# Part of the inverse's correction on TensorE sums, shorter scans and moved tests in a gated recurrence with a mixture of experts

## The chip, the cores and the metric

The kernel runs on one core of a Trainium2 chip. The metric is the device time of one launch in microseconds (us). The engines are called PE (TensorE), DVE (VectorE), ACT (ScalarE), POOL (GpSimd) and SP (SyncE, which issues transfers).

## What is computed

First a recurrence over 768 steps for each of 4 x 8 (batch, head) pairs, with a complex gate per step and channel whose magnitude is cut to 0.999; then each token of 384 values goes to its best one of 8 experts.

```python
mag = np.sqrt(a_re * a_re + a_im * a_im)
scale = np.minimum(mag, 0.999) / (mag + 1e-06)
a_re_n, a_im_n = (a_re * scale, a_im * scale)
for t in range(S):                     # S = 768, state 48 x 48, complex
    S_re, S_im = ar * S_re - ai * S_im + kv, ar * S_im + ai * S_re
    y[:, :, t] = np.einsum('bhd,bhde->bhe', q[:, :, t], S_re)
...
h = np.maximum(np.einsum('ecd,edf->ecf', disp, w1), 0.0)
y = np.einsum('ecf,efd->ecd', h, w2)   # top-1 routing, scaled by the gate
```

## The kernel before

**Scan.** The 768 steps are cut into chunks of 96. The 256 rows (batch, head, chunk) form two groups g = 0, 1 of 128 partitions. For each group DVE scans products of the complex gates backward over the 96 steps, in seven blocks j of 8, 16, 16, 16, 16, 16 and 8 steps (`scan_ops`). A step is a `mul` (L221) and an `add` (L232). It is issued as one instruction each (a whole step) where another operation stands between the two, and as two half-width instructions each where not, since the second half then covers the first one's result.

**Norm.** Before block j can be scanned, its gates are normalised (`norm_ops`, eleven operations): xa, squares on ACT (L162) written into the tile `a4`; xb, their sums by PE with the identity (tile `xp`, L135; four passes for eight steps, eight for sixteen); xc, on ACT Ln, Exp and Square for each half (L177 to L179); t5, a scaled copy on ACT (tile `t5n`, L184); then on DVE m (L190, one per half), c1 (tile `c0n`, L193), s (L197), and two mul into `a4` (L202). c1 writes in place into `c0n`, which t5 reads.

**Post.** Of a scanned block `post_ops` makes q and k scaled by the products and by their inverse: wa, squares on ACT (L257); wb, sums on PE (tile `wp`, L135); wc, Ln and Exp on ACT, the reciprocal v0 (L272, L273); kw on DVE (L276); m (L281, one per half), x times v0; nu (L284), (m − 2)·v0, a correction step of the reciprocal; gq (L288), −nu·q; qw (L292), followed by a store to memory by POOL (tile `scr`).

**Order.** `dve_ops` writes DVE's order: during the scan of block j stand the norm of block j+1 (g = 0: of block j+1 and after) and the post of block j−1, at fractions of the block given in `NORM_AT` and `POST_AT`. In the first group ACT's and PE's orders come from the framework. `a4` has three buffers (`p_a4`), shared by the blocks of both groups in turn: norm k+2 takes the buffer of post block k−1. From the second group's start on, 32 attention units (a batch and a chunk) run between the scan steps, with all engines in an order by hand (`SLOT` tables; a unit's operations are placed every 10.25 us of DVE cost). A unit loads the stored q and k (tile `qkc`), transposes on PE, multiplies, carries the state (L385: a copy for the first chunk, an add after). PSUM tag `tr` has two buffers. Then come the routing and the experts, where PE does three passes for each product.

**Tests.** `pend_test` (L312 to L315) and `uncovered` test on DVE whether the values are in the range that the method covers; the flag is used late in the expert part.

Of the kernel before, what the change touches and what calls it, by code (L numbers as in the profile page):

```python
# [18 lines left out]
C = 96  # L19
# [22 lines left out]

# [17 lines left out]


class Att:


    def __init__(self, const, c_att, tc, dram, ident, q, k, v, a_re, a_im):
# [142 lines left out]
    def scan_ops(self, g, j):  # L208

        nc = self.nc  # L210
        ops = []
        for s in range(SIZES[j] - 1, -1, -1):
            st = {}

            def mul(cs=slice(0, D), s=s, st=st):
                a4 = self.a4[g, j]
                if 'xy' not in st:
                    st['xy'] = self.p_t.tile([128, 4, D], F32, tag="xy", name=f"xy_{g}_{j}_{s}")
                w = a4[:, s + 1, 0:2, cs]
# [17 lines left out]
            ops += [(mul, lambda f=mul: halves(f), .27), (add, lambda f=add: halves(f), .16)]  # L237
        return ops


    def post_ops(self, g, j):
# [49 lines left out]
        def qw():  # L291
# [36 lines left out]
    def unit(self, b, c):  # L328
# [49 lines left out]
        def add():  # L378

            if not last:  # L380
# [54 lines left out]
    def slots(self):  # L435
# [8 lines left out]
        for n in range(-2, len(us) + 3):  # L444
            for i, (t, o) in enumerate(SLOT if n < ALONE - 1 else SLOT_A if n < ALONE else SLOT_B):
                if 0 <= n + o < len(us):
                    ops.append((n + i / len(SLOT), us[n + o][t], cost.get(t, 0)))
        return ops

    def dve_ops(self, slots, t0, dt):  # L450
# [9 lines left out]
        for k, (g, j) in enumerate(sl):  # L460
# [772 lines left out]
def uncovered(nc, const, sums, smalls, route, out):  # L1233


    bad = const.tile([128, 5], F32, name="bad")
    nc.vector.memset(bad, 0.0)
    for g in range(2):
        ok = const.tile([128, 2, NSUM], F32, name=f"ok{g}")
        sv = sums[g]  # L1240
        nc.vector.tensor_scalar(out=ok[:, 0], in0=sv[:, 0], scalar1=1e5, scalar2=None, op0=ALU.is_lt)
        nc.vector.tensor_scalar(out=ok[:, 1], in0=sv[:, 1], scalar1=1e4, scalar2=None, op0=ALU.is_lt)
        m = const.tile([128, 1], F32, name=f"okm{g}")
        nc.vector.tensor_reduce(out=m, in_=ok.rearrange("p z j -> p (z j)"), op=ALU.min, axis=AX.X)
        nc.vector.tensor_tensor(out=m, in0=m, in1=smalls[g], op=ALU.mult)
        nc.vector.tensor_scalar(out=bad[:, g:g + 1], in0=m, scalar1=-1.0, scalar2=1.0, op0=ALU.mult, op1=ALU.add)
    m = const.tile([C, 1], F32, name="okf")
    nc.vector.tensor_reduce(out=m, in_=route.fine, op=ALU.min, axis=AX.X)
    nc.vector.tensor_scalar(out=bad[:C, 2:3], in0=m, scalar1=-1.0, scalar2=1.0, op0=ALU.mult, op1=ALU.add)
    nc.vector.tensor_reduce(out=bad[:C, 3:4], in_=route.over, op=ALU.max, axis=AX.X)  # L1250
    nc.vector.tensor_reduce(out=bad[0:1, 4:5], in_=route.narrow, op=ALU.max, axis=AX.X)
    one = const.tile([128, 1], F32, name="one")
    nc.vector.memset(one, 1.0)
# [11 lines left out]
def kernel(ctx, tc, q, k, v, a_re, a_im, w_gate, w1, w2, out):  # L1265
# [6 lines left out]
    with ExitStack() as c_main, ExitStack() as c_att:  # L1272
# [102 lines left out]
```

## Time and profile before

| | before |
|---|---|
| runs, us | 674.98, 675.65, 678.44 (median 675.65) |
| profiled execution, us | 671.0, its span 669.3 |
| mean granted PE clock | 0.92 of full |
| busy of the span | PE 81%, DVE 72%, ACT 52%, POOL 14% |
| chain that ended last, by engine | PE 60%, DVE 23%, ACT 8%, DMA 4% |

Rows of a timeline give the start in the span, the duration, the line, the operation, what it writes and reads, and in brackets the idle time before it and what ended that. Times on one engine overlap by some hundredths: what an instruction costs is the distance from its start to the next one's. PE passes that follow each other are shown as one row (x8). The granted clock is in parts of the full 2.4 GHz; .50 is the lower level of 1.2 GHz. A window's row gives its bounds and length, the busy time and (x count) of each engine, the clock, and the transfers' share and GB/s.

The scan of the first group takes the first 130 us, that of the second with its attention units some 170 more, the experts the rest.

### The profile page before, as it was taken

Reading aid. Unit: us, or ns where it says so; the run is one execution under the profiler, and the core shown is the slowest. Engines: PE = TensorE matmul, PEld = TensorE weight load, DVE = VectorE, ACT = ScalarE, POOL = GpSimd, SP = SyncE. Lnnn points to the kernel's source line nnn. Section 1 sums busy time; section 2 is a strip of 40 time slices with the busy share of each in tenths; the row PEclk is TensorE's granted clock in tenths of the full one; section 3 lists DMA queues with packets and bytes.
Section 4 is the critical chain, followed back from the end, with each engine's and each line's share of the span. In section 5 each row is a group of like instructions: output and inputs, shape, how many; then the busy total and the mean of one; then the engine's idle time right before and its main releaser. Section 6 shows DMA issues by size and latency. Waiting matters only on the chain.

```text
span 669.3 us, 12570 instructions
## 1 busy us (share of the span) xinstructions
PE 544.7 (81%) x4455; PEld 472.1 (71%) x4455; DVE 479.7 (72%) x1428; ACT 345.4 (52%) x789; POOL 92.8 (14%) x140
## 2 busy tenths in 40 slices
PE   0344434248798999899999999999999999999994
PEld 0122212126587877789999888899999999999993
DVE  5999999999999999827657776465455545564531
ACT  7456534476788886544554553244444443443420
POOL 8030000000000000101322221101120202021111
PEclk9776656676899999989999999999999999999998
DMA  5299444596659777776988742583535362636101
GB/s 189 66 319 324 165 165 138 192 224 201 193 163 252 189 180 223 248 152 160 217 228 226 179 111 70 156 252 92 171 94 176 104 182 92 201 88 200 35 35 35
DMA packets 73239, 111.89 MB, mean 167 GB/s; under 512 B 6402, under 2 KB 63045, under 8 KB 71888
## 3 DMA queue, kind: packets, MB, share of 16 engines
q1 hardware_dynamic: 66384, 77.13, 42.7%
q0 software_dynamic: 6784, 33.88, 15.0%
q8 instruction: 37, 0.61, 0.4%
q14 instruction: 34, 0.28, 0.1%
HBM read 72.99 MB, written 34.26 MB: 160 GB/s over the span
## 4 chain that ended last, share of the span: by engine, by line
PE 60%; DVE 23%; ACT 8%; issue 4%; DMA 4%; POOL 1%; SPq 0%; POOLq 0%; DVEq 0%; ACTq 0%
PE ph L981 15%; PE my L989 14%; DVE xy L221 5%; PE tr L354 4%; PE pa L362 4%; DVE a L232 4%; PE s L375 3%; PE y L418 3%; DVE qko L292 2%; PE x L610 2%; PE y L423 2%; DVE a L202 2%; PE xp L135 2%; PE my L1003 2%; PE wp L135 2%
## 5 line engine op out<-in xcount | busy, mean ns | idle before, releaser
L135 PE MATMUL xp<-a,ident 128*128 128x384 f32 x84 | 48.2, 739 | 90.2 <-ACT a L162 90.2
L880 DVE TENSOR_TENSOR lo<-raw,hi 128x384 fp32r<-128x384 f32 (+2 forms) x128 | 66.5, 553 | 65.5 <-ACT hi L879 55.9
L135 PEld LDWEIGHTS xp<-a,ident 128*128 128x128 f32 x84 | 23.0, 289 | 110.1 <-ACT a L162 78.3
L879 ACT CAST hi<-raw 128x384 fp32r<-128x384 f32 (+2 forms) x128 | 60.0, 512 | 55.1 <-PE ph L981 42.5
L221 DVE TENSOR_TENSOR xy<-a 128x96 f32<-128x96 f32 (+1 forms) x299 | 74.6, 279 | 0.6
L354 PE MATMUL tr<-ident,qkc 96*96 96x96 f32 x512 | 65.6, 252 | 11.0 <-DMA qkc<-scr 6.9
L981 PE MATMUL ph<-xh,hi 128*128 128x448 f32 (+4 forms) x192 | 69.7, 365 | 1.1 <-DVE hl L1027 0.9
L981 PE MATMUL ph<-xl,hi 128*128 128x448 f32 (+4 forms) x192 | 67.8, 353 | 0.0
L981 PE MATMUL ph<-xh,lo 128*128 128x448 f32 (+4 forms) x192 | 67.7, 353 | 0.0
L1027 DVE SCALAR_TENSOR_TENSOR hl<-ph,hh 128x448 fp32r<-128x448 f32 (+4 forms) x64 | 37.4, 586 | 39.0 <-ACT hh L1026 37.9
L1026 ACT ACTIVATE hh<-ph 128x448 fp32r<-128x448 f32 (+4 forms) x64 | 32.8, 514 | 61.0 <-PE ph L981 60.6
L989 PE MATMUL my<-hl,hi 128*128 128x448 f32 (+4 forms) x168 | 60.2, 358 | 0.0
L354 PEld LDWEIGHTS tr<-ident,qkc 96*96 96x96 f32 x512 | 47.6, 129 | 17.5 <-issue 6.7
L989 PE MATMUL my<-hh,lo 128*128 128x448 f32 (+4 forms) x168 | 59.9, 356 | 0.0
L989 PE MATMUL my<-hh,hi 128*128 128x448 f32 (+4 forms) x168 | 56.1, 360 | 0.1
L232 DVE TENSOR_TENSOR a<-xy 128x48 f32<-128x48 f32 (+1 forms) x296 | 55.1, 215 | 0.4
L362 PE MATMUL pa<-qT,kT 128*96 128x96 f32 x512 | 54.8, 251 | 0.0
L362 PEld LDWEIGHTS pa<-qT,kT 128*96 128x96 f32 x512 | 50.6, 168 | 1.4 <-issue 1.0
L954 POOL DMA_INDIRECT out_dram<-o,xr x26 | 28.9, 1111 | 157.7 <-DVE o L953 155.9
L630 POOL DMA_INDIRECT disp<-x,idx x32 | 30.1, 939 | 116.5 <-DVE idx L629 64.7
L418 PE MATMUL y<-a_sb,v 128*64 128x96 f32 x512 | 42.3, 253 | 2.3 <-ACT lt L621 1.7
L375 PE MATMUL s<-v,qkc 128*96 128x96 f32 x448 | 44.1, 253 | 0.0
(196 smaller groups left out, 1187.4 us busy)
## 6 DMA issues: line engine op xcount, KB each, us to landing
raw<-in_moe_w_dram SPq DMA_DIRECT2D x64, 384.0 KB
qkc<-scr SPq DMA_DIRECT2D x32, 528.0 KB
scr<-qko POOLq DMA_DIRECT2D x10, 1536.0 KB, 6.9
disp<-fill POOLq DMA_DIRECT2D x7, 772.0 KB, 17.6
v<-in_v_dram SPq DMA_DIRECT2D x32, 144.0 KB
xr<-disp SPq DMA_DIRECT2D x6, 675.5 KB
sx<-s SPq DMA_DIRECT2D x56, 72.0 KB
a<-in_a_re_dram SPq DMA_DIRECT2D x10, 384.0 KB
```

The costliest lines, as they stand in the source:

```text
L135: nc.tensor.matmul(out=pt[:, :m], lhsT=self.ident, rhs=t[:, h:h + m], start=i == 0, stop=i == 1)
L221: nc.vector.tensor_tensor(out=st['xy'][:, :, cs].rearrange("p (u z) d -> p u z d", u=2), in0=crossed(a4[:, s, 1, cs]), in1=w, op=ALU.mult)
L232: nc.vector.tensor_tensor(out=o, in0=xy[:, 0:4:2, cs], in1=xy[:, 1:4:2, cs], op=ALU.add)
L354: nc.tensor.transpose(out=pt[:, h * C:h * C + C], in_=qk(slice(0, C), 4 * hh + h, slice(z_ * C, z_ * C + C)), identity=self.ident[:C, :C])
L362: nc.tensor.matmul(out=pa[:, h * C:h * C + C], lhsT=kT[:, 4 * hh + h], rhs=qT[:, 4 * hh + h], start=True, stop=True)
L375: nc.tensor.matmul(out=ps[:, h * D:h * D + C], lhsT=qk(slice(None), h, slice(C, 2 * C)), rhs=v[:, h * D:h * D + C], start=True, stop=True)
L418: nc.tensor.matmul(out=py[o:o + DP, i // 2 * C:i // 2 * C + C], lhsT=v[:, h * D:h * D + DP], rhs=a_sb[:, h, :], start=True, stop=c == 0)
L879: nc.scalar.copy(out=hi[i][:, s], in_=raw[i][:, s])
L880: nc.vector.tensor_tensor(out=lo[i][:, s], in0=raw[i][:, s], in1=hi[i][:, s].bitcast(F32), op=ALU.subtract)
L981: nc.tensor.matmul(out=ph[:, :WIDTHS[e]], lhsT=a[:, k, fs], rhs=r[:, k, :WIDTHS[e]], start=k == 0 and i == 0, stop=k == KT - 1 and i == 2)
L989: nc.tensor.matmul(out=py[m][:, :WIDTHS[e]], lhsT=a[:, f % self.PF, ms], rhs=r[:, :WIDTHS[e]], start=f == 0 and i == 0, stop=f == NF - 1 a ...
L1027: nc.vector.scalar_tensor_tensor(out=hl[:, :w], in0=ph[:, :w], scalar=0.0, in1=hh[:, :w].bitcast(F32), op0=ALU.max, op1=ALU.subtract)
```

## The change

In the first group nu is made by PE: into a PSUM tile `nu` of tag `tr` go −2·v0 (with a new constant matrix `minus2`) plus m by the identity, where m is now x·v0². ACT makes v0² by a new Square for each half. gq reads PSUM in two halves. The second group keeps DVE's nu.

In block 0 of both groups the first scan step falls away, as its factor is one: the step after reads the swapped values, and two ACT copies write what stood there. The fractions for the first group are new, and some of the second's. `pend_test(0)` goes from the second group's first block to the end of the scans; the range tests go from before the experts into the expert part, where the flag is summed; the state copy of a first chunk goes from DVE to ACT (four of them); the unit spacing is 10.1.

```diff
-NORM_AT = [(-.25, -.15, .012, .012, .43, .25, .376, .45, .52, .611, .711)] * NS + \
+NORM_AT = [(-.25, -.15, .012, .012, .52, .472, .503, .535, .628, .66, .691)] * NS + \
...
-POST_AT = [(0, .138, .138, 0, .42, .421, .55, .55, .68)] * NS + \
+POST_AT = [(0, .138, .138, .441, .566, .597, .61, .722, .753, .785)] * NS + \
...
+        self.minus2 = const.tile([128, 128], F32, name="minus2")
+        nc.gpsimd.tensor_scalar(out=self.minus2, in0=self.ident, scalar1=-2.0, scalar2=None, op0=ALU.mult)
...
-        for s in range(SIZES[j] - 1, -1, -1):
+        top = SIZES[j] - 1
+        for s in range(top - (j == 0), -1, -1):
+            turned = j == 0 and s == top - 1
...
-                w = a4[:, s + 1, 0:2, cs]
+                w = swapped(a4[:, s + 1, 1, cs]) if turned else a4[:, s + 1, 0:2, cs]
...
+                if turned and cs.start == 0:
+                    a = self.a4[g, j][:, top]
+                    nc.scalar.copy(out=a[:, 0], in_=a[:, 1])
+                    nc.scalar.mul(out=a[:, 1], in_=a[:, 2], mul=-1.0)
...
+                if sums:
+                    nc.scalar.activation(st['o'][:, i, 0, 1], v0[:, i], AF.Square)
...
-                nc.vector.tensor_tensor(out=st['m'][:, i], in0=x, in1=st['v0'][:, i], op=ALU.mult)
+                nc.vector.tensor_tensor(out=st['m'][:, i], in0=x, in1=st['o'][:, i, 0, 1] if sums else st['v0'][:, i], op=ALU.mult)
+
+        def nu_sums():
+            st['nu'] = []
+            for x, i in st['xs']:
+                pt = self.ps.tile([128, 8, D], F32, tag="tr", name=f"nu_{g}_{j}_{i.start}", bufs=2)
+                m = i.stop - i.start
+                nc.tensor.matmul(out=pt[:, :m], lhsT=self.minus2, rhs=st['v0'][:, i], start=True, stop=False)
+                nc.tensor.matmul(out=pt[:, :m], lhsT=self.ident, rhs=st['m'][:, i], start=False, stop=True)
+                st['nu'].append((pt[:, :m], i))
+
+        def gq_of(k):
+            for x, i in st['nu'][k:k + 1]:
+                nc.vector.scalar_tensor_tensor(out=st['v0'][:, i], in0=x, scalar=-1.0, in1=st['in'][:, 0, i],
+                                               op0=ALU.mult, op1=ALU.mult)
...
-                    nc.vector.tensor_copy(out=ss, in_=psv)
+                    nc.scalar.copy(out=ss, in_=psv)
...
-                at.append((0.56, .8, lambda: (self.pend_copy(0), self.pend_test(0), self.pend_cols(0))))
+                at.append((0.56, 0, lambda: (self.pend_copy(0), self.pend_cols(0))))
...
-        out += [lambda: self.pend_copy(1), lambda: self.pend_test(1), lambda: self.pend_cols(1)]
+        out += [lambda: self.pend_copy(1), lambda: self.pend_test(1), lambda: self.pend_test(0), lambda: self.pend_cols(1)]
...
-                ops = att.dve_ops(slots, 6.5, 10.25)
+                ops = att.dve_ops(slots, 6.5, 10.1)
```

DVE, the last part of scan block 2 of the first group, before, with c1 of norm 3 (`c0n_3`) and the end of post block 1 (`qko_1`, `v_0_1`):

```order
L193 SCALAR_TENSOR_TENSOR c0n_3_397<-lnn_3_396,c0n_3_397 128x768
L221 TENSOR_TENSOR xy_2_7_464<-a_0_2_211 128x192
L197 SCALAR_TENSOR_TENSOR t5n_3_398<-c0n_3_397,t5n_3_398 128x768
L232 TENSOR_TENSOR a_0_2_211<-xy_2_7_464 128x96
L284 SCALAR_TENSOR_TENSOR v_0_1_425<-qko_1_393,v_0_1_425 128x768
L221 TENSOR_TENSOR xy_2_6_470<-a_0_2_211 128x192
L288 SCALAR_TENSOR_TENSOR v_0_1_425<-v_0_1_425,qkin_1_252 128x768
L232 TENSOR_TENSOR a_0_2_211<-xy_2_6_470 128x96
L202 TENSOR_TENSOR a_0_3_364<-a_3_263,t5n_3_398 128x16x48
L221 TENSOR_TENSOR xy_2_5_476<-a_0_2_211 128x4x24 x2
L232 TENSOR_TENSOR a_0_2_211<-xy_2_5_476 128x2x24 x2
L292 TENSOR_TENSOR qko_1_393<-a_0_1_152,v_0_1_425 128x16x96
```

The same part after the change:

```order
L206 SCALAR_TENSOR_TENSOR c0n_3_394<-lnn_3_393,c0n_3_394 128x768
L236 TENSOR_TENSOR xy_2_6_467<-a_0_2_209 128x192
L303 TENSOR_TENSOR qko_1_391<-wp_1_0_416,qko_1_391 128x8x48
L251 TENSOR_TENSOR a_0_2_209<-xy_2_6_467 128x96
L303 TENSOR_TENSOR qko_1_391<-wp_1_8_419,qko_1_391 128x8x48
L236 TENSOR_TENSOR xy_2_5_479<-a_0_2_209 128x192
L210 SCALAR_TENSOR_TENSOR t5n_3_395<-c0n_3_394,t5n_3_395 128x768
L251 TENSOR_TENSOR a_0_2_209<-xy_2_5_479 128x96
L215 TENSOR_TENSOR a_0_3_361<-a_3_262,t5n_3_395 128x16x48
L236 TENSOR_TENSOR xy_2_4_485<-a_0_2_209 128x192
L215 TENSOR_TENSOR a_0_3_361<-a_3_262,t5n_3_395 128x16x48
L251 TENSOR_TENSOR a_0_2_209<-xy_2_4_485 128x96
```

and right behind these:

```order
L316 SCALAR_TENSOR_TENSOR v_0_1_422<-nu_1_0_473,qkin_1_250 128x384
L236 TENSOR_TENSOR xy_2_3_491<-a_0_2_209 128x192
L316 SCALAR_TENSOR_TENSOR v_0_1_422<-nu_1_8_476,qkin_1_250 128x384
L251 TENSOR_TENSOR a_0_2_209<-xy_2_3_491 128x96
L328 TENSOR_TENSOR qko_1_391<-a_0_1_154,v_0_1_422 128x16x96
```

Both m (now L303) have moved behind `c0n`, nu is gone, and gq (L316) is two instructions that read `nu_1`; qw (L328) is the last of the stretch, as L292 is before.

ACT, norm 3 and post block 1, from the last Ln of xp to t5, before:

```order
L177 ACTIVATE lnn_3_396<-xp_3_8_376,b_tiny 128x384
L178 ACTIVATE c0n_3_397<-lnn_3_396,b_lncap 128x384
L272 ACTIVATE v_0_1_425<-wp_1_0_419,b_tiny 128x384
L179 ACTIVATE lnn_3_396,sums_82<-c0n_3_397 128x384
L273 ACTIVATE v_0_1_425<-v_0_1_425 128x384
L272 ACTIVATE v_0_1_425<-wp_1_8_422,b_tiny 128x384
L273 ACTIVATE v_0_1_425<-v_0_1_425 128x384
L184 ACTIVATE t5n_3_398<-c0n_3_397,b_half 128x768
L204 ACTIVATE a_0_3_364<-a_0_3_364 128x16x48
```

and after the change:

```order
L190 ACTIVATE lnn_3_393<-xp_3_8_374,b_tiny 128x384
L191 ACTIVATE c0n_3_394<-lnn_3_393,b_lncap 128x384
L292 ACTIVATE v_0_1_422<-wp_1_0_416,b_tiny 128x384
L192 ACTIVATE lnn_3_393,sums_84<-c0n_3_394 128x384
L293 ACTIVATE v_0_1_422<-v_0_1_422 128x384
L292 ACTIVATE v_0_1_422<-wp_1_8_419,b_tiny 128x384
L295 ACTIVATE qko_1_391<-v_0_1_422 128x8x48
L293 ACTIVATE v_0_1_422<-v_0_1_422 128x384
L295 ACTIVATE qko_1_391<-v_0_1_422 128x8x48
L197 ACTIVATE t5n_3_395<-c0n_3_394,b_half 128x768
L217 ACTIVATE a_0_3_361<-a_0_3_361 128x16x48
```

Two Squares (L295) into `qko_1` now stand between the first Exp of v0 (L293) and t5 (`t5n_3`, now L197).

PE, the end of the first group (`wp_5` and `nu_6` belong to its last two post blocks, `xp_1` and `xp_2` to norms 1 and 2 of the second group, `pt` is made by pend_cols), before:

```order
L135 MATMUL wp_5_0_917<-qko_5_897,ident 128x384 x2
L135 MATMUL wp_5_8_920<-qko_5_897,ident 128x384 x2
L135 MATMUL xp_1_0_985<-a_1_1_976,ident 128x384 x2
L135 MATMUL xp_1_8_988<-a_1_1_976,ident 128x384 x2
L324 MATMUL pt_0_1038<-ident,pend_130 96x128
L324 MATMUL pt_1_1041<-ident,pend_130 96x128
L135 MATMUL xp_2_0_1053<-a_1_2_1046,ident 128x384 x2
```

and after the change:

```order
L148 MATMUL wp_5_0_930<-qko_5_911,ident 128x384 x2
L148 MATMUL wp_5_8_933<-qko_5_911,ident 128x384 x2
L310 MATMUL nu_5_0_973<-v_0_5_936,minus_79 128x384
L310 MATMUL nu_5_8_976<-v_0_5_936,minus_79 128x384
L311 MATMUL nu_5_0_973<-qko_5_911,ident 128x384
L311 MATMUL nu_5_8_976<-qko_5_911,ident 128x384
L148 MATMUL xp_1_0_1008<-a_1_1_996,ident 128x384 x2
L148 MATMUL xp_1_8_1011<-a_1_1_996,ident 128x384 x2
L310 MATMUL nu_6_0_1041<-v_0_6_1000,minus_79 128x384
L311 MATMUL nu_6_0_1041<-qko_6_994,ident 128x384
L363 MATMUL pt_0_1051<-ident,pend_132 96x128
L363 MATMUL pt_1_1054<-ident,pend_132 96x128
```

The sums of `nu_6` stand behind both halves of `xp_1`.

## Rows read from the trace of the kernel before

**Rows 1.** Windows of 20 us. Columns: window, us, then PE, PEld, DVE, ACT, POOL busy, PEclk.
```profile
20.00:40.00 20.00, 6.55 (x14) 3.24 (x13) 19.82 (x83) 10.41 (x18) 5.58 (x8) 0.66 0.45 149
...
100.00:120.00 20.00, 7.96 (x16) 3.50 (x15) 19.89 (x75) 9.62 (x18) 0.75 (x3) 0.71 0.40 138
...
180.00:200.00 20.00, 19.31 (x193) 15.25 (x192) 19.39 (x53) 17.12 (x47) 0.00 (x0) 0.92 0.66 205
...
320.00:340.00 20.00, 20.00 (x284) 18.39 (x283) 11.57 (x29) 10.82 (x27) 6.13 (x7) 1.00 0.93 229
```

**Rows 2.** Timeline of DVE, one scan block of the first group. Columns: start us, us, instruction.
```profile
51.67 1.75 DVE L292 TENSOR_TENSOR qko<-a,v 128x1536 f32<-128x1536 f32 x1
...
60.00 0.42 DVE L221 TENSOR_TENSOR xy<-a 128x96 f32<-128x96 f32 x2
...
60.59 0.42 DVE L221 TENSOR_TENSOR xy<-a 128x96 f32<-128x96 f32 x2
...
64.29 0.35 DVE L221 TENSOR_TENSOR xy<-a 128x192 f32<-128x192 f32 x1
64.55 0.55 DVE L281 TENSOR_TENSOR qko<-wp,v 128x384 f32<-128x384 f32 x1
65.02 0.25 DVE L232 TENSOR_TENSOR a<-xy 128x96 f32<-128x96 f32 x1
65.25 0.96 DVE L193 SCALAR_TENSOR_TENSOR c0n<-lnn,c0n 128x768 f32<-128x768 f32 x1
...
66.40 0.95 DVE L197 SCALAR_TENSOR_TENSOR t5n<-c0n,t5n 128x768 f32<-128x768 f32 x1
67.27 0.25 DVE L232 TENSOR_TENSOR a<-xy 128x96 f32<-128x96 f32 x1
67.44 0.95 DVE L284 SCALAR_TENSOR_TENSOR v<-qko,v 128x768 f32<-128x768 f32 x1
...
71.06 1.75 DVE L292 TENSOR_TENSOR qko<-a,v 128x1536 f32<-128x1536 f32 x1
```

**Rows 3.** Timeline of ACT, the same block.
```profile
53.45 1.48 ACT L162 ACTIVATE a<-a 128x1536 f32<-128x1536 f32 x1 [1.41 <-DVE qko L292]
...
63.87 0.52 ACT L273 ACTIVATE v<-v 128x384 f32<-128x384 f32 x1
64.30 0.92 ACT L184 ACTIVATE t5n<-c0n,b_half 128x768 f32<-128x768 f32 x1
```

**Rows 4.** Timeline of PE, xp and wp of the first group and norm 1's after it.
```profile
55.08 5.47 PE L135 MATMUL xp<-a,ident 128*128 128x384 f32 x8 [11.85 <-ACT a L162]
60.36 2.76 PE L135 MATMUL wp<-qko,ident 128*128 128x384 f32 x8
...
74.47 4.32 PE L135 MATMUL xp<-a,ident 128*128 128x384 f32 x8 [11.34 <-ACT a L162]
...
111.18 2.93 PE L135 MATMUL xp<-a,ident 128*128 128x384 f32 x4 [9.22 <-ACT a L162]
...
128.63 4.54 PE L135 MATMUL xp<-a,ident 128*128 128x384 f32 x8 [11.04 <-ACT a L162]
```

**Rows 5.** Timeline of DVE, boundary of the groups.
```profile
125.22 1.75 DVE L292 TENSOR_TENSOR qko<-a,v 128x1536 f32<-128x1536 f32 x1
...
132.82 0.25 DVE L312 TENSOR_TENSOR psq<-pend 128x96 f32<-128x96 f32 x1
...
133.70 0.25 DVE L232 TENSOR_TENSOR a<-xy 128x96 f32<-128x96 f32 x1
...
136.09 0.96 DVE L193 SCALAR_TENSOR_TENSOR c0n<-lnn,c0n 128x768 f32<-128x768 f32 x1
```

**Rows 6.** Timeline view's summary of line 385: ns min/median/max, first and last start us.
```profile
L385 DVE COPY s<-s x2: 546/546/547, 158.3 to 171.2; 96x384 f32<-96x384 f32 x2
```

**Rows 7.** A window of 2.5 us between two blocks, columns as in rows 1.
```profile
67.50:70.00 2.50, 0.00 (x0) 0.00 (x0) 2.50 (x6) 0.00 (x0) 0.00 (x0) 0.50 0.00 0
```

**Rows 8.** Timeline of PE, second group.
```profile
285.90 0.84 PE L354 MATMUL tr<-ident,qkc 96*96 96x96 f32 x4 [3.54 <-DMA qkc<-scr]
```

More of the change, by code (lines that the diff above doesn't have):

```diff
@@ L28 @@
 DM = H * D
-NORM_AT = [(-.25, -.15, .012, .012, .43, .25, .376, .45, .52, .611, .711)] * NS + \
+NORM_AT = [(-.25, -.15, .012, .012, .52, .472, .503, .535, .628, .66, .691)] * NS + \
           [(-.108, .058, .058, .18, .18, .313, .371, .395, .47, .47, .55)] * NS
-NORM_AT[1] = (-.2, -.081, -.081, -.081, -.081, .44, .45, .57, .655, .7, .752)
-NORM_AT[NS + 1] = (.002, .1, .241, .4, .4, .6, .83, .883, .883, .883, .955)
+NORM_AT[1] = (-.2, -.081, -.081, -.081, -.081, .503, .514, .651, .749, .8, .859)
+NORM_AT[2] = NORM_AT[2][:8] + (.597, .628, .66)
+NORM_AT[NS - 1] = NORM_AT[NS - 1][:4] + (.5, .472, .485, .503, .597, .628, .66)
+NORM_AT[NS] = (-.108, .058, .058, .18, .18, .44, .45, .51, .57, .635, .82)
+NORM_AT[NS + 1] = (.002, .1, .241, .4, .4, .68, .9, .95, .95, .95, .99)
 NORM_AT[NS + 2] = (-.42, -.2) + NORM_AT[NS + 2][2:6] + (.41, .43) + NORM_AT[NS + 2][8:]
@@ L37 @@
 NORM_AT[NS + 4] = NORM_AT[NS + 4][:6] + (.42, .45) + NORM_AT[NS + 4][8:]
-POST_AT = [(0, .138, .138, 0, .42, .421, .55, .55, .68)] * NS + \
+POST_AT = [(0, .138, .138, .441, .566, .597, .61, .722, .753, .785)] * NS + \
           [(.015, .354, .354, .18, .58, .647, .7, .7, .8)] * NS
-POST_AT[NS - 2] = (0, .138, .138, 0, .48, .56, .62, .62, .72)
-POST_AT[NS - 1] = (0, .041, .042, .021, .39, .39, .45, .5, .54)
+POST_AT[0] = POST_AT[0][:7] + (.691, .691, .722)
+POST_AT[NS - 3] = POST_AT[NS - 3][:4] + (.535, .566, .58, .691, .722, .753)
+POST_AT[NS - 2] = (0, .138, .138, .38, .69, .755, .76, .88, .945, .95)
+POST_AT[NS - 1] = (0, .041, .042, .021, .39, .39, .4, .6, .6, .62)
 SLOT = [("S", 0), ("L", 2), ("M0", -1), ("T1", 1), ("R3", -3), ("G", -2), ("M1", -1), ("X", -2), ("D", 0),
@@ L59, in crossed, with swapped @@
     return bass.AP(a.tensor, a.offset, [list(p), [-D, 2], [D, 2], list(d)])
+def swapped(a):
+    p, d = a.ap
+    return bass.AP(a.tensor, a.offset, [list(p), [-D, 2], list(d)])
 class Att:
@@ L211, in scan_ops, with mul @@
         ops = []
-        for s in range(SIZES[j] - 1, -1, -1):
+        top = SIZES[j] - 1
+        for s in range(top - (j == 0), -1, -1):
             st = {}
-            def mul(cs=slice(0, D), s=s, st=st):
+            turned = j == 0 and s == top - 1
+            def mul(cs=slice(0, D), s=s, st=st, turned=turned):
                 a4 = self.a4[g, j]
@@ L222, in mul, with add @@
                                         in0=crossed(a4[:, s, 1, cs]), in1=w, op=ALU.mult)
-            def add(cs=slice(0, D), s=s, st=st):
+            def add(cs=slice(0, D), s=s, st=st, turned=turned):
+                if turned and cs.start == 0:
+                    a = self.a4[g, j][:, top]
+                    nc.scalar.copy(out=a[:, 0], in_=a[:, 1])
+                    nc.scalar.mul(out=a[:, 1], in_=a[:, 2], mul=-1.0)
                 if s > 0:
@@ L246, in post_ops @@
         st = {}
+        sums = g == 0
         def load():
@@ L299, in qw @@
                     nc.gpsimd.dma_start(out=self.scr[g][0][bl * 64:bl * 64 + 64], in_=o[bl * 64:bl * 64 + 64])
+        if sums:
+            return load, [wa, wb, wc, kw, lambda: m(0), lambda: m(1), nu_sums, lambda: gq_of(0), lambda: gq_of(1), qw], \
+                [0, 0, 0, n * .104, .46, .46 * (n > 8), 0, .46, .46 * (n > 8), n * .104]
         return load, [wa, wb, wc, kw, lambda: m(0), lambda: m(1), nu, gq, qw], [0, 0, 0, n * .104, .46, .46 * (n > 8)] + [n * c for c in (.054, .054, .104)]
@@ L446, in slots @@
                 if 0 <= n + o < len(us):
-                    ops.append((n + i / len(SLOT), us[n + o][t], cost.get(t, 0)))
+                    ops.append((n + i / len(SLOT), us[n + o][t], 0 if t == "D" and (n + o) % 16 < 2 else cost.get(t, 0)))
         return ops
@@ L1233, in uncovered @@
 def uncovered(nc, const, sums, smalls, route, out):
[L1236 to L1253, printed above, removed]
+    keep = route.tc.keep_in_program_order
@@ L1254, in uncovered @@
     total = const.tile([1, 1], F32, name="flagf")
     def flag(ps):
+        bad = const.tile([128, 5], F32, name="bad")
+        nc.gpsimd.memset(bad, 0.0)
+        one = const.tile([128, 1], F32, name="one")
+        nc.gpsimd.memset(one, 1.0)
+        for g in range(2):
+            ok = const.tile([128, 2, NSUM], F32, name=f"ok{g}")
+            sv = sums[g]
+            keep(nc.vector.tensor_scalar(out=ok[:, 0], in0=sv[:, 0], scalar1=1e5, scalar2=None, op0=ALU.is_lt))
+            keep(nc.vector.tensor_scalar(out=ok[:, 1], in0=sv[:, 1], scalar1=1e4, scalar2=None, op0=ALU.is_lt))
+            m = const.tile([128, 1], F32, name=f"okm{g}")
+            nc.vector.tensor_reduce(out=m, in_=ok.rearrange("p z j -> p (z j)"), op=ALU.min, axis=AX.X)
+            nc.vector.tensor_tensor(out=m, in0=m, in1=smalls[g], op=ALU.mult)
+            nc.vector.tensor_scalar(out=bad[:, g:g + 1], in0=m, scalar1=-1.0, scalar2=1.0, op0=ALU.mult, op1=ALU.add)
@@ L1257, in flag @@
+        m = const.tile([C, 1], F32, name="okf")
+        keep(nc.vector.tensor_reduce(out=m, in_=route.fine, op=ALU.min, axis=AX.X))
+        nc.vector.tensor_scalar(out=bad[:C, 2:3], in0=m, scalar1=-1.0, scalar2=1.0, op0=ALU.mult, op1=ALU.add)
+        keep(nc.vector.tensor_reduce(out=bad[:C, 3:4], in_=route.over, op=ALU.max, axis=AX.X))
+        keep(nc.vector.tensor_reduce(out=bad[0:1, 4:5], in_=route.narrow, op=ALU.max, axis=AX.X))
         pb = ps.tile([128, 512], F32, tag="tr", name="pbad", bufs=2)
```

## The prediction

> **What bounds the kernel now.** I read the busy windows first. From 20 to 120 us VectorE (DVE) is busy 19.8 us or more of every 20 (five windows; first and last shown, with TensorE (PE) at 6.6 and 8.0 and ScalarE (ACT) at about half); from 180 us PE and DVE are both above 19, and at 320 us PE has all 20 and DVE 11.6 [rows 1]. So DVE looks like the limit of the first group, both engines of the second, PE of the expert layer.
>
> The timelines of one scan block say more. On DVE, `qw` of post block 0 begins at 51.67 and ends at 53.42 [rows 2]. At 53.45 ACT starts xa of norm 3 (L162), after an idle time that this qw ended [rows 3]: a4 has three buffers (p_a4), and norm 3 writes into the one whose values this qw was the last to read. PE idles 11.85 us for this xa, and its eight xp passes then take 5.47; the next eight, on wp, take 2.76 [rows 4]. On ACT the last Exp of v0 begins at 63.87, t5n runs from 64.30 to 65.22 [rows 3], and DVE's c0n, which overwrites what t5n reads, begins at 65.25 [rows 2]. The next qw ends at 71.06 + 1.75 = 72.81. **This is a loop**: qw to xa to xp to t5n to c0n to qw, 72.81 − 53.42 = 19.39 us a block. t5n ends 11.80 after qw, c0n to qw takes 7.56. DVE's own work just fills the 11.80, so DVE shows no idle time, but it has no slack over the loop either. What shortens DVE alone shortens nothing here, unless the loop is shortened too.
>
> **The change, part by part.** In the first group a block's c0n-to-qw stretch gets longer. Before, it held c0n, the scale s, nu, gq, one mul and qw; now c0n stands ahead of both `m`, so the stretch holds c0n, two m, s, two mul, two gq halves, qw, and four whole scan steps. Prices: a 128x768 operation advances DVE by 66.40 → 67.27 = .87 (c0n, s and the muls are taken at this), a half-sized one by 64.55 → 65.02 = .47 (it reads PSUM, as the new gq does), a whole scan step by .26 (64.29 to 64.55) + .17 (67.27 to 67.44) [rows 2]. Sum: 4 × .87 + 4 × .47 + 1.75 + 4 × .43 = **8.83**, against 7.56.
>
> ACT's chain also gets longer: the two new Squares (L295) stand ahead of t5n in ACT's order. A half-sized activation advances ACT by 63.87 → 64.30 = .43 [rows 3], so t5n ends .85 later. The nu passes on PE wait on ACT and DVE only after xp has run, and cost nothing in the loop as long as they end before the next xp; they do, by about 7 us.
>
> Period after, with xp 5.47: 11.80 + .85 + .03 + 8.83 = 21.51. The xp passes took 4.32 in the next block [rows 4], which gives 20.36. I take the middle, 20.94: **+1.55 a block, +4.65 over the three full blocks** (norms 3 to 5). Bounds: 3 × (20.36 − 19.39) = +2.9 and 3 × (21.51 − 19.39) = +6.4. DVE's own work per block falls to about 18.3 (nu and gq, .87 each, become two gq of .47; two more steps are whole), so DVE will now wait some 2.7 us ahead of c0n.
>
> The two blocks after them have eight-wide norms: four xp passes, 2.93 us at 111.18 [rows 4]. Their loop is shorter by some 2.5 us, so DVE's work counts: the gq saving of .80 comes through in one, and little in the other. I take −.9 for both; bounds −2.4 (all of DVE's saving) and +1.1 (the loop still binds).
>
> At the **boundary to the second group** the order on PE decides. nu of the last post block stands behind the eight passes of xp_1, and DVE's gq, qw and everything after wait for it. Before, from qw_5's end (125.22 + 1.75 = 126.97) to c0n of norm 1 (136.09) was 9.12 us [rows 5]. Now: xa and its release 1.66 (128.63 − 126.97), xp 4.54 (its own row [rows 4]), two nu passes at the slow rate of xp (5.47 / 8 = .68 each) 1.4, then gq .47, qw .87, two m of .47 and the scan steps between, together 3.47: 11.07, so **+1.95**; bounds +1.75 (nu passes faster) and +2.9 (xp 5.47). The removed pend_test here, four operations between 132.82 and 133.70, .88 us [rows 5], and the dropped first scan step of the second group lie in that wait: nothing gained.
>
> The first group's dropped first step saves a half-sized step (60.00 → 60.59, .59 [rows 2]), but two small ACT copies, each at most the .43 of eight times their elements [rows 3], come into the chain of norm 1: 0 ± .3. In the second group two state copies leave DVE while it is full (.55 each, .47 as they advance [rows 6]) and two small tests: −1.2. Moved filler fractions and the unit spacing there only reorder the same work: 0 ± 1. The flag tests, fourteen small operations, at pend_test's .22 each some 3 us of DVE, move into the expert phase, where DVE is idle 8 us of 20 [rows 1]: 0; without that cover they would cost 3. The other two copies come where DVE has room; the minus2 constant is made on POOL, early: 0.
>
> **Sum:** +4.65 − .9 + 1.95 − 1.2 = +4.5. The profiled execution would go from 671.0 to 675.5 (span 669.3 to 673.8). That execution lies 4.65 below the median of the runs shown, 675.65; on the median the forecast is **680.2**.
>
> **The rivals.** *C: DVE is the limit, as the busy rows say.* Then every operation removed counts: 4.94 for nu and gq over seven blocks (.80 × 5 + .47 × 2), 1.2 for a net eight steps that become whole (.15 each), 1.2 for two first steps, .9 for pend_test, .1 tests, .9 copies: −9.2, **666.4**, faster. The place is c0n in the three full blocks; it decides for C if t5n is done by the time DVE gets there, 18.3 − 8.8 = 9.5 us after qw, against the 12.7 − or 11.5 with the shorter xp − that I work out. For it: DVE has no idle time in the first group. Against it: c0n begins .03 after t5n ends.
>
> By the Trainium skill ("Perfetto Trace Analysis", Identifying the Most-Contended Engine) the engine with the highest occupancy is the bottleneck and is to be optimized first, which is what this change does and would give C's time. The same page (Optimization Strategy, on consistent bubbles) allows that a repeated gap comes from too few buffers (here PE's wait of 11.85 us in every block, which the trace ends with a4's release).
>
> *B: PE's clock stays high through xp.* Then xp takes 2.76 like wp [rows 4], the period is 21.51 − 2.71 = 18.8, three blocks give −1.8, the eight-wide ones −1.5 (between the two values above), the boundary 1.95 − 1.78 − .7 = −.5 (xp and both nu passes at the rate of wp), the rest −1.2: −5.0, **670.7**. For it: the nu passes fall into what was PE's idle time. Against it: they end about 7 us ahead of the next xp, and at 67.50 to 70.00 the granted clock is .50, the lower level (1.2 GHz), with PE's last work over at 63.12 [rows 7, 4]; after 9.22 us of idle time xp still ran at .73 a pass [rows 4].
>
> The Trainium skill ("TensorE: Matmul & The Clock Gate", HAM oscillation) tells of loops whose wait is longer than their compute, where every round starts cold again; the trace agrees (5.47 after 11.85 idle), and by it the added passes do not warm xp.
>
> *D: the loop binds, but later work gives part back.* PE waits in the second group, for example 3.54 us at 285.90 for a transfer [rows 8]; time that the first group loses may come out of such waits, if they don't hang on the first group's stores. Then about half remains past the boundary, and with the second group's −1.2 and shorter spacing the whole is about +1: **676.7**.
>
> *E: the change doesn't do what it says*: the fillers might all fall elsewhere than the fractions suggest. The order of the instructions shows them where the stretch above has them, so it gets no chance.
>
> **How the numbers follow.** My forecast .67, with 678.4 to 682.0 likeliest and 677.4 to 683.4 in all, from the bounds of the three blocks (−1.8, +1.7), the boundary (−.2, +1.0) and the eight-wide pair; D .18; B .06; C .07; .02 for something worse than the bounds. A change within 0.5% (3.4 us) can't be told from none by a measurement of this kernel. Faster takes B, C and a little of D: .14. Within 0.5%, 672.3 to 679.0: most of D and a quarter of the forecast, about .30. Slower: .56. The range 674.0 to 684.5 leaves out B, C and a few in a hundred on either side.
>
> **What would show it.** On DVE idle time before c0n in norms 3 to 5, 1.5 to 3 us each, released by ACT's t5n; qw to qw 20.4 to 21.6 there; two Squares between Exp and t5n; xp at 4.3 to 5.5. At the boundary gq waits for PE, and c0n comes 11 us after qw_5. I am wrong if DVE stays full from 40 to 110 us and qw to qw is 18.3 (C), or if xp takes 2.8 (B), or if the first group ends later by 5 us and the whole isn't (D).

## The result and the profile after

The changed kernel takes 680.86 us (median of 12 runs) against 674.79 before, a ratio of 1.0079 (95% interval 1.0060 to 1.0099): slower, by 5.3 us on that ratio, where +4.5 was forecast. The profiled execution took 679.23 us, its span 677.4, so 8.1 more than the span before. **The forecast number is right, but only the first group's part of its sum is.** Two other terms were wrong, in opposite directions, so that the sum fits by luck: the experts take 4.4 us more where 0 was forecast, and the second group gains more than the 1.2 us forecast. On the ratio the two nearly cancel (5.3 us less 6.1 of the first group and 4.4 of the experts leaves about −5 for the second, an estimate); this pair of traces, 8.1 us apart, shows −2.3 there.

| stretch | before, us | after, us | difference | forecast |
|---|---|---|---|---|
| start to c1 of norm 1, second group | 136.09 | 142.15 | +6.06 | +5.7 |
| from there to the experts' first product (ph) | 282.5 | 280.2 | −2.3 | −1.2 |
| experts, first ph to start of last my | 240.4 | 244.8 | +4.4 | 0 |
| the rest | 10.3 | 10.3 | 0 | 0 |

**First group.** The timeline of DVE of the changed kernel, the block of [rows 2]:

```profile
54.24 1.75 DVE L328 TENSOR_TENSOR qko<-a,v 128x1536 f32<-128x1536 f32 x1
...
68.08 0.96 DVE L206 SCALAR_TENSOR_TENSOR c0n<-lnn,c0n 128x768 f32<-128x768 f32 x1 [2.36 <-ACT t5n L197]
...
74.54 0.56 DVE L316 SCALAR_TENSOR_TENSOR v<-nu,qkin 128x384 f32<-128x384 f32 x1
...
75.17 1.75 DVE L328 TENSOR_TENSOR qko<-a,v 128x1536 f32<-128x1536 f32 x1
```

qw ends at 55.99 and at 76.92: a period of 20.93 us where 20.94 was forecast; c1 to the end of qw is 8.84 (8.83 forecast), and DVE now waits 2.36 us for t5n ahead of c1 (2.7 forecast), in three blocks by the same amount. ACT, the same block, with the two Squares between Exp and t5n:

```profile
65.75 0.51 ACT L295 ACTIVATE qko<-v 128x384 f32<-128x384 f32 x1
66.16 0.51 ACT L293 ACTIVATE v<-v 128x384 f32<-128x384 f32 x1
66.70 0.52 ACT L295 ACTIVATE qko<-v 128x384 f32<-128x384 f32 x1
67.13 0.92 ACT L197 ACTIVATE t5n<-c0n,b_half 128x768 f32<-128x768 f32 x1
```

The idle time shows in DVE's busy windows, which were full before [rows 1] (columns as there):

```profile
60.00:80.00 20.00, 9.93 (x23) 4.59 (x23) 17.45 (x60) 10.94 (x19) 0.54 (x1) 0.84 0.65 242
```

PE, from the same stretch to the boundary of the groups:

```profile
57.66 4.90 PE L148 MATMUL xp<-a,ident 128*128 128x384 f32 x8 [5.83 <-ACT a L175]
...
69.83 1.56 PE L311 MATMUL nu<-qko,ident 128*128 128x384 f32 x4 [2.20 <-DVE qko L303]
...
78.59 4.67 PE L148 MATMUL xp<-a,ident 128*128 128x384 f32 x8 [7.20 <-ACT a L175]
...
131.92 5.31 PE L148 MATMUL xp<-a,ident 128*128 128x384 f32 x8 [6.28 <-ACT a L175]
```

xp still takes 4.7 to 5.3 us, though PE's idle time ahead of it fell from 11.85 [rows 4] to 5.8 to 7.2: nu passes that long before it do not keep the clock up (granted .50 from 57.66 to 60.00 us). At the boundary gq waits for PE:

```profile
128.50 1.75 DVE L328 TENSOR_TENSOR qko<-a,v 128x1536 f32<-128x1536 f32 x1
...
138.55 0.56 DVE L316 SCALAR_TENSOR_TENSOR v<-nu,qkin 128x384 f32<-128x384 f32 x1 [3.51 <-PE nu L311]
...
142.15 0.96 DVE L206 SCALAR_TENSOR_TENSOR c0n<-lnn,c0n 128x768 f32<-128x768 f32 x1
```

From qw_5's end at 130.25 to c1 are 11.90 us (11.07 forecast, 9.12 before [rows 5]).

**Experts.** Here the change edits only the flag tests, and the extra 4.4 us come elsewhere. On ACT, the first weights (raw) of the second expert arrive; before:

```profile
432.45 0.93 ACT L879 CAST hi<-raw 128x512 fp32r<-128x512 f32 x2 [6.24 <-DMA raw<-in_moe_w_dram]
433.28 0.54 ACT L1026 ACTIVATE hh<-ph 128x448 fp32r<-128x448 f32 x1
434.71 1.76 ACT L879 CAST hi<-raw 128x512 fp32r<-128x512 f32 x4 [0.89 <-DMA raw<-in_moe_w_dram]
```

and after:

```profile
437.19 0.93 ACT L918 CAST hi<-raw 128x512 fp32r<-128x512 f32 x2 [7.45 <-DMA raw<-in_moe_w_dram]
439.44 0.92 ACT L918 CAST hi<-raw 128x512 fp32r<-128x512 f32 x2 [1.33 <-DMA raw<-in_moe_w_dram]
440.27 0.54 ACT L1065 ACTIVATE hh<-ph 128x448 fp32r<-128x448 f32 x1
```

The Relu hh, which PE needs, now stands behind the second pair of hi, which waits for its transfer. PE waits for it and comes back at a lower clock (.66 from 440 to 445 us; 1.49 us for three passes):

```profile
440.86 1.49 PE L1028 MATMUL my<-hh,hi 128*128 128x448 f32 x3 [2.96 <-ACT hh L1065]
```

No line of the change says so: outside of the hand-written parts the framework orders ACT and PE, and in the changed kernel it has put this stretch in another order.

### The profile page after: what moved, and what is told of

Read it like the earlier page. It is cut to its first block, busy times and chain, and to the rows that moved or that the text cites. A ratio compares the mean times of both kernels' runs of the same rounds, so it can differ in the third digit from the quotient of the medians.

```text
span 677.4 us, 12676 instructions
## 1 busy us (share of the span) xinstructions
PE 565.5 (83%) x4503; PEld 479.9 (71%) x4503; DVE 471.2 (70%) x1396; ACT 352.6 (52%) x809; POOL 92.6 (14%) x143
## 4 chain that ended last, share of the span: by engine, by line
PE 59%; DVE 21%; ACT 7%; DMA 6%; issue 4%; SPq 1%; POOL 0%; POOLq 0%; DVEq 0%; ACTq 0%
PE ph L1020 15%; PE my L1028 14%; DVE xy L236 4%; PE tr L393 4%; PE pa L401 4%; PE xp L148 3%; PE s L414 3%; DVE a L251 3%; PE y L457 3%; DVE qko L328 2%; DMA qkc<-scr 2%; PE y L462 2%; PE my L1042 2%; PE x L649 2%; DVE a L215 2%
## 5 line engine op out<-in xcount | busy, mean ns | idle before, releaser
L148 PE MATMUL xp<-a,ident 128*128 128x384 f32 x84 | 46.7, 719 | 60.8 <-ACT a L175 60.8
L401 PEld LDWEIGHTS pa<-qT,kT 128*96 128x96 f32 x512 | 49.2, 165 | 2.2 <-issue 1.4
L414 PEld LDWEIGHTS s<-v,qkc 128*96 128x96 f32 x448 | 41.7, 169 | 1.3 <-issue 0.6
```

What stands on the lines that cost most here:

```text
L148: nc.tensor.matmul(out=pt[:, :m], lhsT=self.ident, rhs=t[:, h:h + m], start=i == 0, stop=i == 1)
L401: nc.tensor.matmul(out=pa[:, h * C:h * C + C], lhsT=kT[:, 4 * hh + h], rhs=qT[:, 4 * hh + h], start=True, stop=True)
L414: nc.tensor.matmul(out=ps[:, h * D:h * D + C], lhsT=qk(slice(None), h, slice(C, 2 * C)), rhs=v[:, h * D:h * D + C], start=True, stop=True)
```

## The experiments

Ratios are to the kernel before, with their intervals; c1, ph and the experts' length are read from each run's trace. The second stretch of a single trace scatters by 3 us and more (before: 282.5, and 285.5 in its near-twins c1ln_before and before_hh; 279.2 to 284.9 in runs whose order on DVE is the same from c1 on); the experts' length repeats within 0.5 us for one order.

| run | ratio | c1 of norm 1 | to first ph | experts |
|---|---|---|---|---|
| changed kernel | 1.0079 (1.0060–1.0099) | 142.2 | 280.2 | 244.8 |
| c1ln_after | 0.9941 (0.9917–0.9965) | 134.6 | 282.9 | 242.0 |
| c1ln_before | 0.9972 (0.9951–0.9992) | 136.7 | 285.5 | 240.4 |
| nu6_dve | 1.0126 (1.0104–1.0149) | 138.7 | 284.7 | 245.8 |
| flags_back | 1.0064 (1.0038–1.0089) | 142.7 | 281.6 | 244.9 |
| hh_first | 1.0007 (0.9989–1.0025) | 141.2 | 279.2 | 239.9 |
| before_hh | 0.9995 (0.9978–1.0012) | 136.9 | 285.5 | 240.0 |
| c1ln_hh | 0.9918 (0.9892–0.9944) | 135.3 | 284.9 | 239.9 |
| rest_hh | 1.0066 (1.0036–1.0095) | 136.9 | 281.4 | 247.4 |
| rest_pinned | 0.9987 (0.9967–1.0006) | 135.6 | 286.6 | 239.9 |
| nu6_pinned | 0.9926 (0.9901–0.9951) | 131.7 | 287.7 | 239.9 |
| a4x4_kept | 0.9975 (0.9954–0.9996) | 137.7 | 281.4 | 240.0 |
| nu6_spaced | 0.9885 (0.9850–0.9920) | 133.2 | 281.9 | 239.9 |

**Cutting the loop at c1** (c1ln_after; the same edit on the kernel before is c1ln_before):

```diff
-nc.vector.scalar_tensor_tensor(out=st['c0'], in0=st['ln'], scalar=-3.0, in1=st['c0'],
+nc.vector.scalar_tensor_tensor(out=st['ln'], in0=st['ln'], scalar=-3.0, in1=st['c0'],
...
-nc.vector.scalar_tensor_tensor(out=st['t5'], in0=st['c0'], scalar=-2.0, in1=st['t5'],
+nc.vector.scalar_tensor_tensor(out=st['t5'], in0=st['ln'], scalar=-2.0, in1=st['t5'],
```

> The changed kernel, with c1 written in place of its other operand (tile ln) instead of c0n, so that nothing on DVE waits for ACT's t5n before the scale s. Loop theory: the stretch behind t5n shrinks from 8.83 to 8.83 - 2.52 (c1, two m, one whole scan step and one half of one) = 6.3 us, the loop is 17.8 to 19.0 us against DVE's own 18.3, so the 2.36 us idle before c1 in norms 3 to 5 is gone, qw to qw falls from 20.7-21.4 to 18.3-19.0 there, and the whole falls by 4 to 7 us, to 674-677. Rival (the idle time on DVE is paid elsewhere anyway, second group or expert part bind): the first group ends 5 us or more earlier and the whole moves by less than 1.5 us.

> The kernel before with the same one edit. Loop theory: before, DVE's own work filled the loop exactly, so cutting the loop gains nothing: qw to qw stays 19.3-19.4, the whole within 1 us of before (674.8). Rival (the loop alone set the period before, DVE's fullness being only apparent): qw to qw falls by up to 1.1 us a block, the whole by 3 us.

In c1ln_after, DVE's timeline has no idle time ahead of c1:

```profile
51.22 1.75 DVE L328 TENSOR_TENSOR qko<-a,v 128x1536 f32<-128x1536 f32 x1
...
62.38 0.95 DVE L206 SCALAR_TENSOR_TENSOR lnn<-lnn,c0n 128x768 f32<-128x768 f32 x1
...
69.46 1.75 DVE L328 TENSOR_TENSOR qko<-a,v 128x1536 f32<-128x1536 f32 x1
...
80.82 0.56 DVE L203 TENSOR_TENSOR lnn<-xp,lnn 128x384 f32<-128x384 f32 x1 [0.76 <-ACT lnn L192]
...
88.54 1.75 DVE L328 TENSOR_TENSOR qko<-a,v 128x1536 f32<-128x1536 f32 x1
```

qw to qw is 18.24 us in the first block shown, DVE's own 18.3 of the forecast. It is 19.08 in the next, where DVE waits .76 us ahead of m, and 18.85 in the one before; without the edit the three were 20.93, 20.71 and 21.37. In c1ln_before it stays at 19.3, so that before the change DVE's own work set the period. The loop lay just under it. On ACT, before:

```profile
44.41 0.92 ACT L184 ACTIVATE t5n<-c0n,b_half 128x768 f32<-128x768 f32 x1
...
82.74 0.92 ACT L184 ACTIVATE t5n<-c0n,b_half 128x768 f32<-128x768 f32 x1
```

and on DVE:

```profile
45.87 0.95 DVE L193 SCALAR_TENSOR_TENSOR c0n<-lnn,c0n 128x768 f32<-128x768 f32 x1
...
84.57 0.95 DVE L193 SCALAR_TENSOR_TENSOR c0n<-lnn,c0n 128x768 f32<-128x768 f32 x1
```

c1 begins .54 and .91 us after the end of t5n in these two blocks, and .03 in the block between them [rows 2, 3]. The loop is confirmed: it had little slack before, and the edit alone takes the changed kernel below the one before. That it fell by more than expected (1.4% by the ratios, 9.3 us) has a second reason: its expert part got 2.8 us shorter, because the framework happened to order ACT there as before.

**nu of the last block back on DVE** (nu6_dve):

```diff
-        sums = g == 0
+        sums = g == 0 and j < NS - 1
...
-POST_AT[NS - 1] = (0, .041, .042, .021, .39, .39, .4, .6, .6, .62)
+POST_AT[NS - 1] = (0, .041, .042, .021, .39, .39, .45, .5, .54)
```

> The changed kernel, with nu of the last block of the first group made on DVE as before (its sums on PE no longer stand behind xp of norm 1). Loop theory: from the end of qw_5 to c1 of norm 1 of the second group falls from 11.9 us to 9.1-9.9, nothing else moves, the whole falls by 1 to 2.8 us. Rival (the second group is held elsewhere and gives it back): the 11.9 falls as well, the whole stays within 0.7 us.

A miss: the boundary shrank as expected (129.0 to 138.7 is 9.7 us), but the whole got slower. In the trace most of the loss is in the second stretch, 284.7 us against 280.2: from c1 on DVE's order is no longer that of the changed kernel but, row for row, that of nu6_pinned below, which is long there too. In the expert part, 1.0 us longer, PE's transposes of the second expert's rows have moved ahead and wait for their transfer:

```profile
435.94 1.20 PE L958 MATMUL mt<-ident,xr 112*128 112x112 f32 x5 [3.94 <-DMA xr<-disp]
```

**Range tests back ahead of the experts** (flags_back: the function `uncovered` as before):

> The changed kernel, with the range tests where they were, ahead of the experts. Theory (moved tests are covered): the expert part, first product to last, stays as long as in the changed kernel's profile or is as jittery, and the whole stays within 1 us of 680.9. Rival (they disturb the expert part, which is 4.4 us longer in the changed kernel's profile): the expert part falls by 3 to 4 us and the whole to 677-678.

The expert part stays at 244.9 with the same wait on hh (3.14 us), and the interval of the ratio overlaps that of the changed kernel. The moved tests are not its cause, and no cost of them can be seen, as forecast.

**The order of the experts' first steps kept** (hh_first; before_hh is the control; c1ln_hh has the c1 edit as well):

```diff
-            nc.scalar.activation(hh[:, :w], ph[:, :w], AF.Relu)
+            ins = nc.scalar.activation(hh[:, :w], ph[:, :w], AF.Relu)
+            if s < NF:
+                self.tc.keep_in_program_order(ins)
```

and the same for the copies `hi` of the second expert's first two weight parts and for its copies `xh`.

> The changed kernel, with ACT's Relu (hh) of the first expert's steps, the transposed rows (xh) and the weight splits (hi) of the second expert kept in the order in which the program writes them. Nothing is computed otherwise. In the changed kernel's own order ACT has both pairs of hi ahead of an hh on which PE waits 2.96 us; before, hh stands between the pairs and PE does not wait. Theory (this reordering, a by-product of the change, costs the expert part's extra 4.4 us): PE's 3 us wait is gone, the expert part (first ph to last my) falls from 244.8 to 240-241.5, the whole from 680.9 to 677-678. Rival (the transfers come late whatever the order): the wait moves to another instruction, the expert part stays above 243.5, the whole within 1 us of 680.9.

> The kernel before with the same edit, as its control. Both theories: there was no wait to remove, the expert part stays at 240.4 (up to 1 us more if the program's order is itself worse), the whole within 1 us of before.

> The changed kernel with both edits (c1 in place of tile ln; order of the experts' first steps kept). Theory: the 1.3 us wait that the expert part of the c1 edit alone still had is gone too: 1 to 1.5 us less than that one's 670.9, so 669.4-670, 0.8% below before. Rival (the order edit gains nothing): 670-672.

ACT in hh_first, at the same place: no hh stands behind a waiting hi.

```profile
434.37 0.55 ACT L1069 ACTIVATE hh<-ph 128x448 fp32r<-128x448 f32 x1 [2.91 <-PE ph L1024]
435.50 0.93 ACT L918 CAST hi<-raw 128x512 fp32r<-128x512 f32 x2 [0.59 <-DMA raw<-in_moe_w_dram]
438.03 0.55 ACT L1069 ACTIVATE hh<-ph 128x448 fp32r<-128x448 f32 x1 [1.60 <-PE ph L1024]
```

PE's busy windows there, of the changed kernel:

```profile
430.00:440.00 10.00, 7.90 (x40) 7.03 (x38) 1.42 (x3) 1.49 (x4) 0.00 (x0) 1.00 0.91 272
440.00:450.00 10.00, 9.14 (x39) 8.21 (x40) 6.78 (x13) 5.33 (x13) 0.00 (x0) 0.83 0.79 220
```

and of hh_first:

```profile
430.00:440.00 10.00, 10.00 (x53) 9.20 (x52) 2.90 (x5) 2.71 (x6) 0.00 (x0) 1.00 1.04 337
```

The experts' 4.9 us are gone in the trace, 0.72% (4.9 us) in the ratios, and the control does not move. So **the reordering makes up nearly all of the measured slowdown**: without it the change is at 1.0007, no difference that can be measured. hh_first and c1ln_hh have row for row the same order on DVE; they reach c1 5.9 us apart, and their ratios differ by 0.89%, 6.0 us (about 4 to 8, an estimate from the two intervals). So by the ratios what the first group loses reaches the end. The two traces alone do not show it: both profiled executions took 672 us (672.27 and 672.11), that of c1ln_hh, the slowest of its six, with a second stretch 5.7 us longer.

**The change without its nu part** (rest_hh: `sums = False` and the fractions of before; rest_pinned also keeps PE's transposes `mt` and the first expert's first products in order):

> The changed kernel without its nu part: nu on DVE in both groups, the filler fractions of before, no Squares for v0; what is left of the change are the dropped first scan steps, the moved tests, the state copies on ACT and the unit spacing 10.1. The order of the experts' first steps is kept, as in the control. Loop theory: blocks 2 to 4 of the first group stay at 19.4 us qw to qw, the boundary near 9; the second group gains about 1 us: the whole 0.5 to 2.5 us below the kernel before with the same order edit. Rival (the parts besides nu are what slows the change): slower than the control by 2 us or more.

> The changed kernel without its nu part, as the run before of that kind, and now PE's transposes of the second expert's rows and the first expert's first products also kept in program order, since there they had moved ahead and cost a wait of 4.7 us: the expert part's order is now row for row that of the changed kernel with kept order. Theory: the expert part is 239.9 us as there, blocks 2 to 4 stay at 19.4, and the whole is 2 to 4 us below before (670-671.5): the parts besides nu gain, and the nu part costs what they gain. Rival: within 1 us of before, so that the nu part cost nothing in the end.

rest_hh answers nothing: its expert part had a wait like that of nu6_dve, 4.7 us. Pinned, the rest is at 0.9987, a gain of 0.9 us that is not clear of none: a miss, and the rival's reading. The nu part costs 5.6 us up to c1 (141.2 against 135.6), and yet hh_first is only 0.20% (1.4 us) slower, which is not clear of none either. Something in the second group pays for the difference.

**Boundary and unit spacing** (nu6_pinned: c1 edit, nu of the last block on DVE, all kept orders; nu6_spaced has one number more):

```diff
-                ops = att.dve_ops(slots, 6.5, 10.1)
+                ops = att.dve_ops(slots, 6.9, 10.1)
```

> The changed kernel with the c1 edit, nu of the first group's last block on DVE, and the experts' order kept on ACT and PE, row for row as in the run with kept order. Loop theory on the boundary: end of qw_5 to c1 of norm 1 of the second group falls from 11.9 us to about 9, unit 0's store is issued 4 to 5 us earlier, and of this 1 to 2.5 us reach the end: 665.5-667 against 667.9 of the same without it. Rival (the second group gives it back): 667.5-669.

> The run with the c1 edit, nu of the first group's last block on DVE and all kept orders, with one number more: the first unit's place on DVE is 6.9 us instead of 6.5, which makes DVE's order in the second group row for row that of the c1 edit with kept order (13 rows differ, at the boundary alone; without the number 147 differ all through). Theory (the second group's length hangs on how the units stand between the scan steps: from c1 of norm 1 to the end it was 534 us in the two runs with that order, by trace and median, and 538 in three with the other): boundary at 131.7 us as there, 534 us from it, the whole 665-667.5, 1.2% below before. Rival (the boundary's 3.6 us are given back by whatever waits in the second group): 669-670.5 as without the number.

nu6_pinned is a miss: it reaches c1 3.6 us earlier than c1ln_hh and ends no earlier. DVE's cost in the block at the boundary differs by .4 us in the planner's books, and this shifts all units against the scan steps of the second group. Moved back by that .4, the boundary is at 133.2 us and the ratio 0.9885, the best of all runs, though its interval still touches that of nu6_pinned. Over all runs, the seven traces with this order of units take 281.7 us on average from c1 to the first ph (279.2 to 284.9), the seven with another 284.8 (281.3 to 287.7). An effect of about 3 us is likely, though single traces of one order scatter by up to 5.7. The ratios say the same: 674.79 us times the ratio, less c1, is 533.8 to 535.4 us in the four runs of this order whose experts take 239.9 to 240.0, and 536.2 to 538.7 in the five of another whose experts take 239.9 to 240.4. Which wait in the second group it is stays open.

**A fourth a4 buffer** (a4x4_kept: `p_a4` with bufs=4 and the kept orders of rest_pinned):

> The changed kernel with four a4 buffers instead of three and the experts' order kept, c1 unedited. xa no longer waits for qw. Loop theory: t5n is done long before DVE comes to c1, no idle time before c1, qw to qw falls from 20.8 to DVE's own 18.2-18.5 in blocks 2 to 4 (a cut of the loop at another place than the c1 edit), and the whole falls like with that edit, 4 to 6 us below 673.6: 668-670. Rival (c1's wait comes from ACT's own load, not from qw): idle time before c1 stays above 1 us, qw to qw above 19.5.

A miss: the rival's reading came true. Blocks 2 to 4 take 22.46, 21.17 and 19.42 us from qw to qw, and the wait at c1 stays:

```profile
70.19 0.96 DVE L206 SCALAR_TENSOR_TENSOR c0n<-lnn,c0n 128x768 f32<-128x768 f32 x1 [2.87 <-ACT t5n L197]
```

and on ACT the reason is seen. The framework now puts xa of the next norm ahead of wp's Ln, where it waits for the load of its own input, and t5n stands behind all of it:

```profile
64.60 1.48 ACT L175 ACTIVATE a<-a 128x1536 f32<-128x1536 f32 x1 [4.07 <-DMA a<-in_a_im_dram]
65.99 0.19 ACT L175 ACTIVATION_READ_ACCUMULATOR a<-a 128x1 f32 x1
66.08 0.56 ACT L292 ACTIVATE v<-wp,b_tiny 128x384 f32<-128x384 f32 x1
...
69.24 0.92 ACT L197 ACTIVATE t5n<-c0n,b_half 128x768 f32<-128x768 f32 x1
```

So the buffer's release was the wait that came last, but not the only one that would hold t5n. What neither reading foresaw is the boundary: xa of norm 1 no longer waits for qw_5, and xp comes 1.45 us behind the nu passes and at the high rate.

```profile
128.49 2.85 PE L148 MATMUL xp<-a,ident 128*128 128x384 f32 x8 [1.45 <-ACT a L175]
```

From qw_5's end (131.50) to c1 are 6.2 us here, 11.9 in hh_first, and the whole is 0.32% below hh_first, with intervals that just overlap.

## Why the prediction was right, and where it was not

- **The loop (+4.65): right.** Blocks 2 to 4 give +2.05, +1.54 and +1.41, together +5.0; in the block shown period, stretch and idle time fit within .4 us. Without xp's time and the gap from t5n to c1, the loop took 13.9, 13.9 and 14.1 us before and 16.0 in all three blocks after: 1.9 to 2.1 more, where .85 + 8.83 − 7.56 = 2.12 was forecast. c1ln_after shows that it is the cause. That DVE had no slack over the loop was read from one block (norm 4 with the qw of post block 1, not norm 3 and post block 0 as the prediction names them); the two beside it had .54 and .91 us.
- **The two eight-wide blocks (−.9): mis-sized.** qw to qw fell from 18.04 to 17.06 and from 16.82 to 15.56, together −2.24: DVE's saving counts there nearly in full, the lower bound.
- **The boundary (+1.95): mechanism right, +2.8 measured.** xp took 5.31 us, not the 4.54 of its own row; the upper bound of +2.9 assumed 5.47. The dropped first step, priced 0 ± .3, is no part of this: qw_0 ends .5 later in this trace (34.62, not 34.10), but the first c1 is already that late (8.55, not 8.07), and in hh_first, nu6_dve and flags_back qw_0 ends at 34.12 to 34.20.
- **"Moved filler fractions and the unit spacing there only reorder the same work: 0 ± 1": wrong.** The second group gains 2.3 us in the pair of traces against a forecast of 1.2, and 4.2 in hh_first against rest_pinned (5.6 lost up to c1, 1.4 at the end), which both have the moved copies and tests, so that 0 was forecast. Rival D foresaw that something is given back, but by transfers' waits soaking up a delay; by the ratios of hh_first and c1ln_hh a delay is not soaked up.
- **The step that failed most: the expert part at 0.** I looked only for the edited tests there, and these show no cost (flags_back). The order of the instructions after the change, which was there to be read, shows ACT's hh behind the second hi pair; I compared the orders only in the scans. It cost 4.9 us (hh_first), about the whole measured difference.
- **Rival C** (DVE is the limit, 666.4) is wrong for this change and comes nearer once the loop is cut: of its −9.2 us c1ln_hh has −5.5 and nu6_spaced −7.8 by the ratios. The Trainium skill ("Perfetto Trace Analysis", Identifying the Most-Contended Engine) says to optimize the engine with the highest occupancy first. The trace bears out that DVE was the limit of the first group before (c1ln_before), but with the loop .03 to .91 us behind it and made longer, DVE is at 17.45 of 20 in the changed kernel where it was full. **Rival B** is wrong: xp stayed at the low rate, as the window between two blocks let one expect [rows 7]; it took 2.85 us in a4x4_kept, where it came 1.45 us behind the nu passes.

So the sign rests on a by-product of the change, and the number on two errors that offset each other: that it came out is luck. With the experts' order held fixed, no change would have been the right forecast, and the first group's loss and the second group's gain are what balances.

## What to carry to other kernels

An engine that is always busy may still have no slack over a loop through other engines: look for waits that are met just in time (here by .03 to .91 us), and move or rename the operand that closes the loop before trimming the busy engine. Where a framework orders the engines, compare the whole program's order after any edit, also far from it: the same arithmetic in another order cost 4.9 us in a part that was hardly touched. Pin that order before measuring what the edit itself is worth.

## What was not expected of the hardware

A wait of PE of 2.96 us in the expert part came with more: the three passes behind it took 1.49 us and the granted clock of the window from 440 to 450 us is .83, and the part as a whole got 4.4 us longer. And one more buffer did not shorten the loop's blocks, where t5n was then held by another wait, of 4.07 us on a transfer, but took 5.7 us off the boundary.
